# Sums of x, and bias plus projection product, taken from GpSimd to VectorE beside the MLP

## The chip, the cores and the metric

The kernel runs on one core of a Trainium2 chip. Its five engines have their own instruction queues, each worked through in order: TensorE (PE, with its weight loads as PEld), VectorE (DVE), ScalarE (ACT), GpSimd (POOL) and SyncE (SP, which here only issues transfers). The metric is the device time of one execution in microseconds, as the median of several runs.

## The reference, cut to what matters

The input x holds 8 batches of 3008 rows with 256 columns. Each batch goes through a real Fourier transform along the rows, a complex linear layer, a soft threshold and the inverse transform; all rows then go through a two-layer MLP of width 2048.

```python
X = np.fft.rfft(x, axis=1)
Yr = Xr @ w_r - Xi @ w_i + b_r
Yi = Xr @ w_i + Xi @ w_r + b_i
Yr = np.sign(Yr) * np.maximum(np.abs(Yr) - lam, 0.0)   # Yi the same
y = np.fft.irfft(Yr + 1j * Yi, n=3008, axis=1)
h = y.reshape(24064, 256) @ w_in
out = np.maximum(0.01 * h, h) @ w_out
```

## The kernel before

The transform of length 3008 is split into 47 times 64. For a batch `b` there are three parts.

`fwd(b)` does the transform of length 47. It loads x in 7 column groups of 512 (the last 256): two tiles `xa` and `xb` of 120 rows each, the second holding the mirrored rows. `fold(c)` makes the sum (into the tile `xs`) and the difference (in place of `xa`), L249 and L250. For batches 2 to 7, `split` then cuts each of the two into a rounded high part and a rest (`xz`, L258 and L259, on VectorE), `stage_a` multiplies on TensorE, ScalarE copies the product from PSUM, and ScalarE's queue stores it into DRAM (`u_dram`). Two groups are loaded ahead. Batch 0 folds on VectorE, batch 1 has no fold at all (`stage_a1`), so the fold runs on GpSimd for batches 2 to 7: 6 times 7 groups, 84 instructions.

`mid(b)` does the transform of length 64 (`stage_b`), the linear layer (`proj`), the threshold and the first part of the way back (`stage_g`), in 12 pairs per batch. In `proj` three products are made; the first (`ps_k`, of `w_r`) serves both the real and the imaginary part. ScalarE copies it to `kc` (L379), and GpSimd adds it, repeated twice, to the two bias rows: `kb` (L381). Later VectorE adds `kb` to the other two products (`t`, L389), and the threshold follows (L390, L391). This runs 12 times in each of 8 batches, 96 times in all; 84 of these belong to batches 1 to 7.

The MLP works through 47 chunks of 512 rows, in 8 steps each, 376 steps in all. A step has `moe_a` (four products into two PSUM banks of tag `psh`), then the second layer of two steps earlier (`moe_o`, in two halves), then `moe_b` (three more products into the same banks). Between them VectorE has to take sums from those banks: L542 (which needs ScalarE's copy `p1`, L541), L544 and L545 after `moe_a`, L556 after `moe_b`; ScalarE's activations (L555, L558) and cast (L560) and VectorE's L562 then make the operands of the second layer. The first matmul of each product in `moe_b` waits for the reader of what it adds to: the last for L545. Between the steps a chunk's operands are made from the inverse transform (`inverse`, L479 to L492) and `forms` (L504 to L512).

What sets the order: the program emits MLP half steps, and after each the spectral work of the next batches (`fwd(b+1)`, then `mid(b)`) up to the share that is due. A list scheduler with a time model of its own then fixes each engine's queue. The MLP's parts are tied to follow one another on TensorE; the spectral work is placed between them. The first batch's `mid(0)` and `fwd(1)` run ahead of the MLP, in about the first 200 us. Buffers: `xs` has one buffer under the tag `e`, shared with `mid`'s operand; `psf` has two PSUM banks for all spectral products; `kb` has one buffer, which `c` of the threshold also uses.

Of the kernel before, what the change touches and what calls it, by code (L numbers as in the profile page):

```python
# [8 lines left out]
F32 = mybir.dt.float32  # L9
# [11 lines left out]
P = 128  # L21
# [9 lines left out]
def spectral_mlp_kernel(  # L31
# [18 lines left out]
    D = w_r.shape[0]  # L50
# [13 lines left out]
    sb = ctx.enter_context(tc.tile_pool(name="sb", bufs=2))  # L64
    dram = ctx.enter_context(tc.tile_pool(name="dram", bufs=2, space=bass.MemoryType.DRAM))
    ps = ctx.enter_context(tc.tile_pool(name="ps", bufs=1, space=bass.MemoryType.PSUM))
    sync, act, dve, pool = nc.sync, nc.scalar, nc.vector, nc.gpsimd

    def bank(tag, bufs):
        return ps.tile([P, 512], F32, name=tag, tag=tag, bufs=bufs)  # L70

    def products(dst, pairs):

        terms = []
        dst = dst.rearrange("p (s b a) -> p s b a", a=2, b=P)
        for l, r in pairs:
            terms += [(l[0], r[0]), (l[0], r[1]), (l[1], r[0])] if len(l) == 2 else [(l[0], r[0])]
        for i, (a, b) in enumerate(terms):
            b = b.rearrange("p (s a b) -> p s b a", a=2, b=P)
            last = nc.tensor.matmul(dst, a, b, start=(i == 0), stop=(i == len(terms) - 1))  # L80
        return last
# [16 lines left out]
    def flat(t):  # L98
        return t.rearrange("p a b -> p (a b)")
# [120 lines left out]
    def fwd(b):  # L220
        ud = dram.tile([2, NK1, NG * NS, D], F32, name="u_dram", tag="u_dram", bufs=NPRE + 1)
        u_dram[b] = ud
        uv = ud.rearrange("c k (g s) d -> c (k g) (s d)", g=NG)
        x_t, s_t = {}, {}

        def load(c):
            cols = slice(2 * c * D, min(2 * c + 2, NS) * D)
            n = cols.stop - cols.start
            if b < NPRE:
                tag, bufs = (XT, XT1)[b][c]  # L230
                x2 = sb.tile([PA, 2, 2 * D], F32, name="xin", tag=tag, bufs=bufs)
                x_t[c] = [x2[:, h, :n] for h in range(2)]
            else:
                x_t[c] = [
                    sb.tile([PA, 2 * D], F32, name=f"xin{h}", tag="uv"[h], bufs=3 - h)[:, :n] for h in range(2)
                ]
            for h, t in enumerate(x_t[c]):
                if b == 0:
                    (act if h else sync).dma_start(t, x[b, h, :, cols])
                else:  # L240
                    with tc.issue_after(reads[-1].ins):
                        sync.dma_start(t, x[b, h, :, cols])

        def fold(c):
            xa, xb = x_t[c]
            n = xa.shape[1]
            eng = pool if b else dve
            xs = sb.tile([PA, 2 * D], F32, name="xs", tag="e", bufs=1)[:, :n] if b else xs3[:, c % 3, :n]
            eng.tensor_add(xs, xa, xb)  # L249
            eng.tensor_sub(xa, xa, xb)  # L250
            s_t[c] = [(xs,), (xa,)] if b < NPRE else [xs, xa]

        def split(c, h):
            t = s_t[c][h]
            n = t.shape[1]
            z = sb.tile([PA, 2, 2 * D], F32R, name="xz", tag="z", bufs=1)
            xh, xl = z[:, 0, :n], z[:, 1, :n]
            dve.tensor_copy(xh, t)  # L258
            dve.tensor_sub(xl, t, xh.bitcast(F32))  # L259
            s_t[c][h] = (xh, xl)  # L260

        def stage_a(c, h):
            t = x_t[c][h]
            n = t.shape[1]
            pa = (bank("psf", 2) if b else bank("psh", 4))[:PA, :n]
            products(pa, [(consts[f"fa{h}"] if b else consts[f"fa{h}32"], s_t[c][h])])
            t = x_t[c][1 - h]
            cp = act.copy(t, pa)
            if b == 0:
                turned[:] = [cp]  # L270
            st = (act if b else sync).dma_start(uv[h, :, 2 * c * D:2 * c * D + n], t)
            if b == 0:
                written.append(st)

        def stage_a1(c):

            n = x_t[c][0].shape[1]
            pas = [(bank("psf", 2) if c in (4, 5) else bank("psh", 4))[:PA, :n] for _ in range(2)]
            for h in range(2):
                with tc.issue_after(turning[NPAIR - 2].ins):  # L280
                    products(pas[h], [
                        (consts[f"fa{h}32"], (x_t[c][0],)), (consts[f"fa{2 * h}32"], (x_t[c][1],))])
            for h in range(2):
                act.copy(x_t[c][h], pas[h])
                sync.dma_start(uv[h, :, 2 * c * D:2 * c * D + n], x_t[c][h])

        if b == 1:
            for c in range(NX):
                load(c)
                yield 0  # L290
            for c in (0, 1, 2, 3, 6, 4, 5):
                stage_a1(c)
                yield 6 * x_t[c][0].shape[1]
            return

        ahead = 2 if b >= NPRE else NX
        for c in range(ahead):
            load(c)
        yield 4 * CS if b >= NPRE else 0
        fold(0)  # L300
        if b >= NPRE:
            split(0, 0)
        yield 0
        for c in range(NX):
            for h in range(2):
                if h == 0 and c + ahead < NX:
                    load(c + ahead)
                if h == 0 and c + 1 < NX:
                    fold(c + 1)
                stage_a(c, h)  # L310
                if b >= NPRE and (c + h < NX):
                    split(c + h, 1 - h)
                yield 3 * x_t[c][h].shape[1]


    def mid(b):
# [49 lines left out]
        def proj(j):  # L366

            e = e_t.pop(j)
            ps_k = bank("psf", 2) if b else bank("pso", 2)
            ps_y = None if b else bank("psf", 2)  # L370
            for dst, c, w in ((0, 2, "wr"), (0, 1, "wn"), (D, 0, "wd")):
                if c == 1 and b:
                    ps_y = bank("psf", 2)
                products((ps_k if c == 2 else ps_y)[:, dst:dst + D], [
                    (tuple(t[:, a, c, :] for t in e), tuple(t[:, a, :] for t in consts[w]) if b else (consts[w + "32"][0][:, a, :],)) for a in range(NH)
                ])
                if c == 2:
                    kc = sb.tile([P, D], F32, name="kc", tag="kc")
                    act.copy(kc, ps_k[:, :D])  # L379
                    kb = sb.tile([P, 2, D], F32, name="kb", tag="kb", bufs=1)  # L380
                    pool.tensor_add(kb, bias, kc.unsqueeze(1).broadcast_to([P, 2, D]))  # L381
                if c:
                    yield 6 * D
                if c == 2 and b and j:
                    stage_g(j - 1)
                    yield 3 * CS
            t = sb.tile([P, 2, D], F32, name="t", tag="t" if b else "v", bufs=1 if b else 2)
            c = sb.tile([P, 2, D], F32, name="c", tag="kb" if b else "yt", bufs=1)
            dve.tensor_add(flat(t), ps_y, flat(kb))  # L389
            dve.tensor_scalar(c, t, LAMBDA, -LAMBDA, ALU.min, ALU.max)  # L390
            thresholded.append(dve.tensor_sub(t, t, c))  # L391
            zf = z0[j % 3] if b == 0 else sb.tile([P, 2, D], F32, name="zf", tag="zf", bufs=1)
            for i in range(2):
                s = slice(64 * i, 64 * (i + 1))
                act.copy(zf[:64, i, :], t[s, 0, :])
                if b == 0 and j == NPAIR - 1:
                    dve.tensor_scalar(zf[64:, i, :], t[s, 1, :], sign[s, NK1 + j:NK1 + j + 1], None, ALU.mult)
                else:
                    act.mul(zf[64:, i, :], t[s, 1, :], sign[s, NK1 + j:NK1 + j + 1])  # L399
            if b == 0:  # L400
                z_t[j] = (zf,)
                yield 6 * D
                return
            z = sb.tile([P, 2, 2, D], F32R, name="zh", tag="z", bufs=1)
            zh, zl = z[:, 0], z[:, 1]
            act.copy(zh, zf)
            dve.tensor_sub(zl, zf, zh.bitcast(F32))
            z_t[j] = (zh, zl)
            yield 6 * D
# [14 lines left out]
        if b:  # L424
            for s in range(NPAIR):
                if s + 2 < NPAIR:
                    load(s + 2)
                stage_b(s)
                yield 16 * P
                yield from proj(s)  # L430
            stage_g(NPAIR - 1)
            yield 3 * CS
            return
# [240 lines left out]
    bias = const.tile([P, 2, D], F32, name="bias")  # L674
# [166 lines left out]
```

## Time and profile before

Times and the profiled execution:

| | |
|---|---|
| median of 3 runs | 2502.09 us (2500.66 to 2505.65) |
| profiled execution | 2500.07 us, its span 2498.3 us |
| mean granted TensorE clock | 0.995 |
| PE busy | 2431.1 us, 97% |
| VectorE busy | 1896.1 us, 76% |
| ScalarE busy | 1659.1 us, 66% |
| GpSimd busy | 255.3 us, 10%, 192 instructions |

The span is the time from the first to the last instruction on the core; the execution's own time has 1.8 us around it. A busy share is over the whole span. "Idle before" is the time that an engine stood still ahead of an instruction, put down to what released it last.

### The profile page before, as it was taken

To read this page: it belongs to the slowest core of one execution; us is meant where nothing else is said; L and a number is where in the kernel's file an instruction comes from. 1 tells how busy PE (TensorE), PEld (TensorE's weight loads), DVE (VectorE), ACT (ScalarE), POOL (GpSimd) and SP (SyncE) were. 2 spreads that over 40 slices of the span, in tenths; PEclk is the share of its full clock that TensorE was granted. 3 is DMA by queue.
4 is the path that set the end of the run, shared out by engine and by line. 5 is a ranking of instruction groups with operands and counts; after the bars stand their busy time and mean duration, and the time that the engine had idled before them with its cause. 6 is when DMAs were issued, how large, how long until landed. Compare 5 with 4: busy or idle time off the path is not lost.

```text
span 2498.3 us, 42605 instructions
## 1 busy us (share of the span) xinstructions
PE 2431.1 (97%) x16276; PEld 2230.4 (89%) x16276; DVE 1896.1 (76%) x3400; ACT 1659.1 (66%) x3172; POOL 255.3 (10%) x192
## 2 busy tenths in 40 slices
PE   6989999999999999999999999999999999999999
PEld 4579988999889999999999999889999899999998
DVE  7687778777777778777787777877778777777775
ACT  5667765776657776576766777667776677656564
POOL 1200112000110101100011000201002010000000
PEclk8999999999999999999999999999999999999999
DMA  8531123211231113221132111321113211101000
GB/s 272 148 107 50 55 67 96 66 53 42 74 91 56 51 38 88 82 61 47 43 93 82 47 55 39 105 70 51 51 35 109 69 55 51 50 18 33 9 18 18
DMA packets 119904, 165.12 MB, mean 66 GB/s; under 512 B 13597, under 2 KB 69909, under 8 KB 119701
## 3 DMA queue, kind: packets, MB, share of 16 engines
q1 hardware_dynamic: 79112, 115.54, 15.0%
q10 hardware_dynamic: 40589, 46.87, 7.3%
q8 instruction: 128, 2.10, 0.4%
q14 instruction: 75, 0.61, 0.1%
HBM read 86.60 MB, written 75.76 MB: 65 GB/s over the span
## 4 chain that ended last, share of the span: by engine, by line
PE 84%; DVE 7%; ACT 4%; DMA 2%; issue 2%; ACTq 0%; POOL 0%; SPq 0%; DVEq 0%; POOLq 0%
PE pso L576 35%; PE psh L96 32%; PE psf L80 11%; PE psf L479 3%; PE psf L347 2%; PE psh L80 1%; DVE yl L505 1%; DMA u_dram<-xin 1%; DVE gl L562 1%; ACT gf L558 1%; ACT zf L399 1%; DMA u<-u_dram 1%; DVE t L389 0%; DVE gf L545 0%; DVE gf L556 0%
## 5 line engine op out<-in xcount | busy, mean ns | idle before, releaser
L96 PE MATMUL psh<-yh,win_hi 128*128 128x256 f32 x2632 | 740.5, 281 | 23.7 <-DVE gf L545 17.7
L96 PE MATMUL psh<-yl,win_hi 128*128 128x256 f32 x2632 | 725.9, 276 | 0.5 <-DVE yl L505 0.5
L96 PE MATMUL psh<-yh,win_lo 128*128 128x256 f32 x2632 | 726.1, 276 | 0.0
L576 PE MATMUL pso<-gh,wout_hi 128*128 128x512 f32 x1504 | 575.1, 382 | 0.1
L576 PE MATMUL pso<-gl,wout_hi 128*128 128x512 f32 x1504 | 571.2, 380 | 0.6 <-DVE gl L562 0.6
L576 PE MATMUL pso<-gh,wout_lo 128*128 128x512 f32 x1504 | 570.3, 379 | 0.0
L96 PEld LDWEIGHTS psh<-yh,win_hi 128*128 128x128 f32 x2632 | 505.9, 192 | 40.5 <-DVE gf L545 23.3
L562 DVE TENSOR_TENSOR gl<-gf,gh 128x1024 fp32r<-128x1024 f32 x376 | 470.2, 1251 | 92.2 <-ACT gh L560 90.1
L96 PEld LDWEIGHTS psh<-yl,win_hi 128*128 128x128 f32 x2632 | 506.0, 192 | 7.2 <-DVE yl L505 0.7
L96 PEld LDWEIGHTS psh<-yh,win_lo 128*128 128x128 f32 x2632 | 506.7, 193 | 0.1
L560 ACT CAST gh<-gf 128x1024 fp32r<-128x1024 f32 x376 | 394.6, 1050 | 7.2
L556 DVE TENSOR_TENSOR gf<-psh,u 128x512 f32<-128x512 f32 x376 | 258.3, 687 | 181.1 <-PE psh L96 180.6
L558 ACT ACTIVATE gf<-gf 128x768 f32<-128x768 f32 x376 | 318.7, 848 | 65.8 <-DVE gf L556 64.1
L576 PEld LDWEIGHTS pso<-gl,wout_hi 128*128 128x128 f32 x1504 | 284.3, 189 | 41.1 <-DVE gl L562 1.5
L576 PEld LDWEIGHTS pso<-gh,wout_hi 128*128 128x128 f32 x1504 | 285.8, 190 | 29.7 <-ACT gh L560 0.5
L576 PEld LDWEIGHTS pso<-gh,wout_lo 128*128 128x128 f32 x1504 | 285.6, 190 | 28.3
L381 POOL TENSOR_TENSOR kb<-bias,kc 128x512 f32<-128x512 f32 x96 | 142.9, 1489 | 1538.7 <-ACT kc L379 1418.1
L555 ACT ACTIVATE gf<-psh 128x256 f32<-128x256 f32 x376 | 145.1, 386 | 230.8 <-PE psh L96 183.9
L541 ACT COPY p<-psh 128x256 f32<-128x256 f32 x376 | 139.7, 372 | 190.7 <-PE psh L96 188.0
L542 DVE TENSOR_TENSOR u<-psh,p 128x256 f32<-128x256 f32 x376 | 157.7, 419 | 100.5 <-ACT p L541 98.9
L544 DVE TENSOR_TENSOR gf<-psh,u 128x256 f32<-128x256 f32 x376 | 158.7, 422 | 29.3 <-PE psh L96 1.6
L545 DVE TENSOR_TENSOR gf<-psh,gf 128x256 f32<-128x256 f32 x376 | 158.6, 422 | 9.0
(126 smaller groups left out, 3242.6 us busy)
## 6 DMA issues: line engine op xcount, KB each, us to landing
u<-u_dram SPq DMA_DIRECT2D x192, 128.0 KB, 2.7
v_dram<-v ACTq DMA_DIRECT2D x192, 128.0 KB, 2.4
out_dram<-ob SPq DMA_DIRECT2D x94, 256.0 KB, 2.2
vin<-v_dram SPq DMA_DIRECT2D x96, 240.0 KB, 3.4
xin<-x_dram SPq DMA_DIRECT2D x90, 240.0 KB, 3.0
u_dram<-xin ACTq DMA_DIRECT2D x72, 240.0 KB, 2.4
u_dram<-xin SPq DMA_DIRECT2D x24, 240.0 KB, 4.6
raw<-w_out_dram SPq DMA_DIRECT2D x8, 512.0 KB, 4.3
```

The source lines that it names most:

```text
L80: last = nc.tensor.matmul(dst, a, b, start=(i == 0), stop=(i == len(terms) - 1))
L96: mlp[:] = [nc.tensor.matmul(dst, a, b, start=start and i == 0, stop=i == 2, skip_group_check=True)]
L381: pool.tensor_add(kb, bias, kc.unsqueeze(1).broadcast_to([P, 2, D]))
L542: dve.tensor_add(u2, b1[:, hi], p1)
L544: dve.tensor_add(g[:, 3], b2[:, hi], u2)
L545: dve.tensor_add(g[:, 3], b2[:, lo], g[:, 3])
L555: act.activation(g[:, 0], b1[:, lo], AF.Prelu, alpha=SLOPE)
L556: dve.tensor_add(g[:, 1:3], b2.rearrange("p (k n) -> p k n", k=2), u2.unsqueeze(1).broadcast_to([P, 2, HT]))
L558: act.activation(g[:, 1:4], g[:, 1:4], AF.Prelu, alpha=SLOPE)
L560: cp = act.copy(gh, g)
L562: parted[:] = [cp, dve.tensor_sub(gl, g, gh.bitcast(F32))]
L576: mlp[:] = [nc.tensor.matmul(pv, a[:, f, s], r[:, i], start=(f == 0 and j == 0), stop=(f == NF - 1 and j == 2),)]
```

## The change

Two edits. `fold` always runs on VectorE. For batches 1 to 7, `kb` is made by one VectorE instruction that reads the product straight from PSUM, and ScalarE's copy `kc` is gone; batch 0 keeps the copy and the add on GpSimd.

```diff
         def fold(c):
             xa, xb = x_t[c]
             n = xa.shape[1]
-            eng = pool if b else dve
             xs = sb.tile([PA, 2 * D], F32, name="xs", tag="e", bufs=1)[:, :n] if b else xs3[:, c % 3, :n]
-            eng.tensor_add(xs, xa, xb)
-            eng.tensor_sub(xa, xa, xb)
+            dve.tensor_add(xs, xa, xb)
+            dve.tensor_sub(xa, xa, xb)
...
                 if c == 2:
-                    kc = sb.tile([P, D], F32, name="kc", tag="kc")
-                    act.copy(kc, ps_k[:, :D])
                     kb = sb.tile([P, 2, D], F32, name="kb", tag="kb", bufs=1)
-                    pool.tensor_add(kb, bias, kc.unsqueeze(1).broadcast_to([P, 2, D]))
+                    if b:
+                        dve.tensor_add(kb, bias, ps_k[:, :D].unsqueeze(1).broadcast_to([P, 2, D]))
+                    else:
+                        kc = sb.tile([P, D], F32, name="kc", tag="kc")
+                        act.copy(kc, ps_k[:, :D])
+                        pool.tensor_add(kb, bias, kc.unsqueeze(1).broadcast_to([P, 2, D]))
```

## Rows read from the trace of the kernel before

**Rows 1.** The page's first part: busy time, share of the span and instructions of each engine.

```profile
PE 2431.1 (97%) x16276; PEld 2230.4 (89%) x16276; DVE 1896.1 (76%) x3400; ACT 1659.1 (66%) x3172; POOL 255.3 (10%) x192
```

**Rows 2.** Busy time in the six stretches in which `fwd(2)` to `fwd(7)` fold. Columns: the stretch and its length in us; busy us and number of instructions of PE, PEld, DVE, ACT, POOL; granted TensorE clock, DMA share, GB/s.

```profile
355.00:430.00 75.00, 73.45 (x470) 66.75 (x469) 62.85 (x103) 46.90 (x82) 20.69 (x14) 1.00 0.36 103
651.00:736.00 85.00, 79.51 (x499) 73.10 (x498) 68.87 (x117) 50.22 (x88) 17.87 (x14) 0.96 0.33 93
965.00:1040.00 75.00, 74.63 (x486) 68.82 (x485) 60.74 (x105) 46.57 (x82) 16.74 (x14) 1.00 0.35 101
1268.00:1345.00 77.00, 76.59 (x495) 70.57 (x495) 62.03 (x107) 48.65 (x84) 17.78 (x14) 1.00 0.35 102
1571.00:1650.00 79.00, 77.43 (x503) 71.13 (x502) 63.33 (x110) 49.91 (x88) 18.71 (x14) 1.00 0.35 102
1879.00:1954.00 75.00, 74.63 (x486) 68.81 (x485) 61.17 (x105) 46.85 (x82) 17.73 (x14) 1.00 0.37 104
```

**Rows 3.** The same view of one stretch in which a `mid` runs beside the MLP, and of the stretch after the last `mid`, in which only the MLP and the inverse transform are left.

```profile
1040.00:1268.00 228.00, 224.95 (x1595) 212.60 (x1594) 173.04 (x323) 159.57 (x319) 17.02 (x13) 1.00 0.18 52
...
2156.00:2400.00 244.00, 244.00 (x1662) 228.98 (x1661) 175.60 (x308) 148.59 (x263) 0.00 (x0) 1.00 0.09 28
```

**Rows 4.** What PE waited for from 200 to 2400 us: us in total, times, longest.

```profile
PE psh L96 <- DVE gf L545: 12.0, 16, 2.8
PE psf L347 <- DMA u<-u_dram: 7.0, 4, 2.0
PE psf L347 <- issue: 4.0, 2, 2.2
PE psh L96 <- DVE u L542: 3.2, 3, 2.1
```

**Rows 5.** Groups of instructions by line and shape over the whole span: count, busy us and mean ns of one, idle time of the engine before them and its releasers.

```profile
L381 POOL TENSOR_TENSOR kb<-bias,kc 128x512 f32<-128x512 f32 x96 | 142.9, 1489 | 1538.7 <-ACT kc L379 1418.1 <-DVE gl L562 82.1 <-DVE yt L508 18.1
...
L389 DVE TENSOR_TENSOR t<-psf,kb 128x512 f32<-128x512 f32 x96 | 65.7, 685 | 25.6 <-POOL kb L381 12.3 <-PE psf L80 11.2 <-PE psh L96 2.0
L391 DVE TENSOR_TENSOR t<-t,c 128x512 f32<-128x512 f32 x96 | 65.7, 685 | 1.3
...
L249 POOL TENSOR_TENSOR xs<-xin,xin 120x512 f32<-120x512 f32 x36 | 47.4, 1316 | 299.0 <-DVE xz L259 126.9 <-DMA xin<-x_dram 54.2 <-DMA vin<-v_dram 33.3
...
L379 ACT COPY kc<-psf 128x256 f32<-128x256 f32 x84 | 31.2, 372 | 16.9 <-PE psf L80 11.8 <-PE psh L96 1.9 <-ACT gf L555 1.7
...
L249 DVE TENSOR_TENSOR xs<-xin 120x512 f32<-120x512 f32 x6 | 4.2, 692 | 8.7 <-DMA xin<-x_dram 8.6
...
L321 POOL MEMSET zero<- 48x256 f32 x8 | 2.4, 304 | 0.7 <-POOLq L828 0.3
```

**Rows 6.** VectorE's groups by line and shape from 200 to 2156 us, in which GpSimd works beside it; columns as in the group before.

```profile
L562 DVE TENSOR_TENSOR gl<-gf,gh 128x1024 fp32r<-128x1024 f32 x302 | 379.7, 1257 | 68.4 <-ACT gh L560 66.5
...
L510 DVE TENSOR_TENSOR yt<-yc,yt 128x256 f32<-128x256 f32 x38 | 20.6, 543 | 2.5 <-ACT yc L492 1.9
L512 DVE TENSOR_TENSOR yc<-yc,yt 128x256 f32<-128x256 f32 x38 | 19.0, 500 | 0.0
```

**Rows 7.** The same groups from 2156 to 2400 us, in which GpSimd does nothing.

```profile
L562 DVE TENSOR_TENSOR gl<-gf,gh 128x1024 fp32r<-128x1024 f32 x47 | 57.5, 1224 | 15.2 <-ACT gh L560 15.0
...
L510 DVE TENSOR_TENSOR yt<-yc,yt 128x256 f32<-128x256 f32 x6 | 2.5, 420 | 0.1
...
L512 DVE TENSOR_TENSOR yc<-yc,yt 128x256 f32<-128x256 f32 x6 | 2.5, 418 | 0.0
```

**Rows 8.** VectorE's instructions in order of time from 651 us on: start us, length us, engine, line, operation, tiles, shape.

```profile
651.25 1.50 DVE L510 TENSOR_TENSOR yt<-yc,yt 128x256 f32<-128x256 f32 x1
652.68 1.48 DVE L511 TENSOR_TENSOR yc<-yc 128x256 f32<-128x256 f32 x1
...
655.68 0.68 DVE L391 TENSOR_TENSOR t<-t,c 128x512 f32<-128x512 f32 x1
656.29 0.68 DVE L505 TENSOR_TENSOR yl<-yt,yh 128x512 fp32r<-128x512 f32 x1
```

**Rows 9.** GpSimd's instructions in the same stretch, with the idle time before them in brackets.

```profile
651.14 1.33 POOL L249 TENSOR_TENSOR xs<-xin,xin 120x512 f32<-120x512 f32 x1 [9.85 <-DMA xin<-x_dram]
652.55 1.33 POOL L250 TENSOR_TENSOR xin<-xin,xin 120x512 f32<-120x512 f32 x1
```

**Rows 10.** What PE waited for from 651 to 660 us.

```profile
PE psh L96 <- DVE gf L545: 2.8, 1, 2.8
PE psh L96 <- DVE u L542: 2.1, 1, 2.1
```

**Rows 11.** Busy time and granted clock (third number from the right) in and behind that wait; columns as in the second group.

```profile
658.00:662.00 4.00, 3.71 (x17) 3.71 (x18) 1.96 (x4) 1.62 (x4) 0.00 (x0) 0.50 0.00 0
...
655.00:664.00 9.00, 6.19 (x29) 5.82 (x30) 6.41 (x13) 5.48 (x10) 0.00 (x0) 0.62 0.01 2
```

**Rows 12.** What GpSimd waited for over the whole span, the fold's transfers alone.

```profile
POOL xs L249 <- DMA xin<-x_dram: 54.2, 6, 9.9
POOL xs L249 <- DMA vin<-v_dram: 33.3, 2, 21.0
```

**Rows 13.** What VectorE waited for from 200 to 2400 us, two rows of it.

```profile
DVE y L483 <- DMA out_dram<-ob: 9.8, 9, 1.6
...
DVE t L389 <- POOL kb L381: 5.0, 6, 0.8
```

## The prediction

> **What bounds the kernel now.** I read the page's busy times first: PE is busy 97% of the span, VectorE 76%, ScalarE 66%, GpSimd 10% [rows 1]. So the time can only fall where PE waits or its clock is low, and rise where PE is made to wait more. Second, the stretches. In the six that fold, PE stands idle 1.55, 5.49, 0.37, 0.41, 1.57 and 0.37 us (length less busy), 9.8 us in all, with VectorE busy 379 of 466 us, 81% [rows 2]. Beside a `mid` PE loses 3.1 us of 228 with VectorE at 76%; with neither, nothing in 244 us at 72% [rows 3]. The reader is to see that PE's losses are small wherever one looks. Third, PE's waits: from 200 to 2400 us, L545 costs 12.0 us in 16 waits and L542 3.2 us in 3; the other large rows are transfers that the change doesn't touch [rows 4]. In 302 steps (the count of L562 [rows 6]) VectorE is thus late 19 times, 6.3%. Last, whether GpSimd has part in them: two VectorE instructions on 256 columns take 1.50 and 1.48 us at 651 us [rows 8], where their mean is 0.42 us without GpSimd [rows 7], and two GpSimd sums run at just that time [rows 9]. PE then waits 2.1 and 2.8 us [rows 10].
>
> **The change part by part.** All terms are made against the profiled execution's own 2500.07 us (span 2498.3 and 1.8 around it); the median of the runs lies 2.0 us above.
>
> *The first 200 us.* Batch 0 keeps its path and batch 1 has no fold, so nothing is added or removed there: 0.
>
> *The folds.* 84 instructions leave GpSimd and come to VectorE: 72 of 512 columns and 12 of 256. VectorE's own fold of batch 0 takes 0.692 us against GpSimd's 1.316 [rows 5]. VectorE starts instructions of that size 0.61 us apart (655.68 to 656.29 [rows 8]), so 72 x 0.61 = 44 us of its queue, and 12 at about half, 4: together 48 us. What goes: the stretching of VectorE by GpSimd. For three lines alone, mean with GpSimd less mean without: L562 (1257 - 1224) x 302 = 10.0 us, L510 (543 - 420) x 38 = 4.7, L512 (500 - 418) x 38 = 3.1: 17.8 us [rows 6, 7]. Other lines add to it, so I take 18 as a lower bound. Net, VectorE gets at most 30 us more in 466 us: (379 + 30) / 466 = 88%. It isn't the bound on average; what counts is how often the extra time lies ahead of an L545 that PE is near to needing. I price this by the share of steps that are late already: 30 x 0.063 = +1.9 us. The bounds are 0 (all of it falls in VectorE's idle time) and 30 (every microsecond passes to PE).
>
> The stretch at 651 us is priced by itself. There 1.08 + 1.06 = 2.1 us of stretch goes, and the pair of sums, whose data has just landed, comes in its place with 2 x 0.61 = 1.2 us: -1.0 us of PE's 4.9 us. Behind the wait the granted clock is 0.50 from 658 to 662 us, the lower of the two levels (1.2 GHz), after PE's two waits [rows 10], and 0.62 from 655 to 664 us [rows 11]: 0.38 x 9 = 3.4 us lost, the idle part counted twice. A shorter wait may or may not keep the clock; bounds 0 and -3.4, I take the middle, -1.7.
>
> *The fold in VectorE's queue.* On GpSimd the fold waits for its load with nothing behind it that matters: 6 times for `xin` itself, 54.2 us, and twice for a transfer ahead of it in the queue [rows 12]. On VectorE everything of the MLP stands behind it. Where the queue's order has the fold before its data has landed, VectorE stops, and L542 to L545 with it. The trace doesn't show this wait. From below it is 0: at 651 us VectorE was busy past the landing. From above, VectorE's nearest wait for a transfer is 9.8 / 9 = 1.1 us [rows 13], PE's for `u` 7.0 / 4 = 1.75 us [rows 4]; with 8 folds, 14 us. I take 0, as at 651 us, and make the other end a rival. The loads themselves are issued by SP in the old order, when a store frees their buffer; nothing is moved past anything there.
>
> *The bias add.* 84 GpSimd instructions (1.489 us each) and 84 ScalarE copies of 0.372 us, 31.2 us, go [rows 5]. VectorE gets 84 adds of 512 columns with one input in PSUM. L389 has just this shape and inputs, 0.685 us, no longer than L391 from SBUF alone [rows 5]. At 0.61 us apart they take 51 us of VectorE over seven `mid`s. By the share of late steps: 51 x 0.063 = +3.2 us (bounds 0 and 51). The PSUM bank is now held until VectorE comes round to the add instead of ScalarE's copy; two yields of other work lie before that bank's next product, so I add nothing for it. Below nothing: ScalarE's 31 us lie ahead of other copies, of which L541 leads to L542. PE's waits for L542 are 3.2 us [rows 4]; I take half as gone, -1.6 (bounds 0 and -3.2). VectorE's 5.0 us of waits for `kb` [rows 13] go too: 5.0 x 0.063 = -0.3.
>
> The Trainium skill ("Perfetto Trace Analysis", Optimizing Scalar/DVE Operations) puts the fixed cost of a VectorE access at about 60 ns for SBUF and 125 ns for PSUM. An estimate from that page would be 84 x 65 ns = 5.5 us more on VectorE, 0.3 us of time by the share above; the equal means of L389 and L391 show none of it.
>
> *What stays.* The memset of 48 rows, 0.30 us, runs once per `mid` on GpSimd [rows 5]; it reads nothing, and I give it 0.
>
> **Sum.** 1.9 - 1.0 - 1.7 + 3.2 - 1.6 - 0.3 = +0.5 us. On the profiled execution 2500.6, on the median 2502.6; the terms are no finer than a microsecond, so I say 2502. Its own range is 2498 to 2506: within it lie the doubled or vanished terms of the queue (5.1 us) with the clock either way.
>
> **The rivals.** *Faster: the order takes the sums in, and the stretch alone was the harm.* The list scheduler knows a VectorE instruction's place in the queue, and need not know of the stretching. Speaking for it: three of six fold stretches already lose only 0.4 us [rows 2], and the three that lose more have 8.6 us of idle time together, 5.5 of them where the two stretched instructions stand. If all six came to 0.4, 9.8 - 2.3 = 7.5 us go, with the clock's 3.4 it is 10.9; with ScalarE's 1.6 gained and half of the bias add's 3.2 paid it stays 10.9: 2502.1 - 10.9 = 2491. Against it: VectorE at 88% beside the folds, where even 72% to 76% is not free of waits.
>
> *Slower: VectorE stops for the fold's load.* Place: the first two folds of each batch, and others whose data lands just in time. Price: 8 stops of 1.75 us, 14 us. Where VectorE lost 2.1 us, PE lost 4.9; take three quarters of the stops as reaching PE, 10.5 us: 2502.1 + 10.5 = 2513 with the sum's remainder. It decides from about 8 us of waits at L249. For it: the loads do land last before their fold. Against it: between the landing and the fold's first use VectorE often has work of the MLP queued.
>
> *Slower: VectorE has too much.* The same page and section of the skill advises to hand work to ScalarE or GpSimd where VectorE is saturated, though it warns that GpSimd shares a read port with it. As a mechanism here: at 88% late steps double in the fold stretches and rise by half beside the `mid`s. PE's 15.2 us of waits [rows 4] would become about 24: 2502 + 9 = 2511. This needs bursts, since no stretch comes to 100%.
>
> *The change does less than it says* is hardly open: both edits name their engine; only the memset stays.
>
> **How the numbers follow.** About 0.2%, 5 us, is what a measurement of this kernel can tell from no change. No change (2502): 0.37. Faster (2491, with its own range 2486 to 2497): 0.35. Slower: 0.28, of which the stop 0.15 and the load 0.13. To leave out no more than two in ten, the range reaches into the middle of both sides: 2489 to 2512.
>
> **What would show it.** Right: GpSimd with 12 adds and 8 memsets left; L510 and L562 at 0.42 and 1.22 us everywhere; VectorE busy near 1896 + 48 + 51 - 18 = 1977 us or somewhat more (busy time counts 0.69 and not 0.61, which adds 12); ScalarE 31 us lower. PE's idle time in the six fold stretches near 8 us, and its waits for L545 near 14. Wrong: a row "DVE xs waits for DMA xin" beyond 8 us (the stop); waits for L545 above 20 us (the load); fold stretches that all lose under 1 us with the clock at 1.00 throughout (the faster case).

## The result and the profile after

The changed kernel takes 2525.19 us (median of 6 runs, 2520.99 to 2527.54) against 2503.81 us of the kernel before: a ratio of 1.0077, 95% interval 1.0067 to 1.0087. It is slower by 0.8%. 2502 us with a range of 2489 to 2512 was predicted; the time lies above the range, and the nearest of the cases is the rival "VectorE stops for the fold's load" (2513). The profiled execution took 2524.32 us, its span 2522.5 us, mean granted clock 0.992.

The page's first part of the kernel after, as in [rows 1]:

```profile
PE 2441.1 (97%) x16276; PEld 2237.0 (89%) x16276; DVE 1955.2 (78%) x3568; ACT 1638.0 (65%) x3088; POOL 23.9 (1%) x24
```

The same 16276 matmuls are busy 10.0 us longer, and the span less PE's busy time has risen from 67.2 to 81.4 us, by 14.2: together the 24.2 us by which the span is longer. Most of the busy part is the clock: 0.5% of 2498.3 is 12.5 us, 0.8% of 2522.5 is 20.2, so 7.7 us more are lost to it (the clock is printed to a thousandth, which leaves 1 to 2 us open).

Where PE stands idle: the six stretches that fold, and the whole steady part (columns as in [rows 2]; the limits are shifted with the kernel's own time).

```profile
355.00:440.00 85.00, 78.42 (x481) 70.56 (x480) 66.14 (x121) 46.83 (x81) 0.00 (x0) 0.96 0.33 95
660.00:745.00 85.00, 78.50 (x492) 70.89 (x491) 70.13 (x129) 49.68 (x89) 0.00 (x0) 0.98 0.33 93
965.00:1053.00 88.00, 87.28 (x569) 80.30 (x569) 75.73 (x138) 55.44 (x98) 0.00 (x0) 1.00 0.33 94
1285.00:1360.00 75.00, 72.88 (x466) 66.30 (x466) 63.85 (x115) 46.40 (x81) 0.00 (x0) 1.00 0.34 96
1590.00:1667.00 77.00, 74.62 (x481) 68.14 (x481) 65.96 (x122) 48.85 (x87) 0.00 (x0) 1.00 0.36 101
1895.00:1972.00 77.00, 75.55 (x487) 68.88 (x486) 65.81 (x120) 46.19 (x81) 0.00 (x0) 1.00 0.35 98
...
200.00:2420.00 2220.00, 2177.55 (x14926) 2035.08 (x14924) 1736.88 (x3198) 1461.23 (x2767) 0.00 (x0) 1.00 0.20 58
```

The stretches lose 6.58, 6.50, 0.72, 2.12, 2.38 and 1.45 us, 19.7 in all, where [rows 2] lost 9.8. (Cut alike in both kernels, from 5 us ahead of a batch's first fold to 10 us behind the start of its last, they lose 16.9 and 9.8.) From 200 to 2420 us PE is idle 2220 - 2177.55 = 42.5 us; the same row of the kernel before:

```profile
200.00:2420.00 2220.00, 2189.77 (x15084) 2050.71 (x15084) 1694.93 (x3056) 1493.94 (x2871) 231.64 (x173) 1.00 0.21 59
```

There it is 30.2. So 12 of the 14 us are lost in the steady part, where the change works. VectorE is no fuller than was forecast: 407.62 of the stretches' 487 us, 84%.

What VectorE waits for from 200 to 2450 us (us in total, times, longest):

```profile
DVE gf L558 <- PE psh L96: 147.2, 149, 3.7
DVE u L544 <- ACT p L543: 81.7, 129, 1.8
...
DVE xs L248 <- DMA xin<-x_dram: 17.6, 7, 4.2
DVE kb L379 <- PE psf L80: 16.9, 19, 1.8
```

Neither of the last two rows has a counterpart before. (Lines have moved: L248 is the fold's first sum, L379 the bias add; L544, L546 and L547 answer to L542, L544 and L545 of before, L558 to L556, L564 to L562.) The first is the row that the prediction named as the sign of the stop, "beyond 8 us".

How one stop looks, VectorE's timeline at 376 us (start, duration, engine, line; in brackets the idle time before):

```profile
376.85 0.68 DVE L258 TENSOR_TENSOR xz<-xs,xz 120x512 fp32r<-120x512 f32 x1
377.44 0.42 DVE L544 TENSOR_TENSOR u<-psh,p 128x256 f32<-128x256 f32 x1
382.06 0.69 DVE L248 TENSOR_TENSOR xs<-xin,xin 120x512 f32<-120x512 f32 x1 [4.20 <-DMA xin<-x_dram]
382.67 0.42 DVE L546 TENSOR_TENSOR gf<-psh,u 128x256 f32<-128x256 f32 x1
383.00 0.68 DVE L249 TENSOR_TENSOR xin<-xin,xin 120x512 f32<-120x512 f32 x1
383.60 0.42 DVE L547 TENSOR_TENSOR gf<-psh,gf 128x256 f32<-128x256 f32 x1
```

The planned order has the batch's second fold between L544 and L546, the sums that free TensorE's banks. The fold stands at the head of the queue for 4.20 us until its load has landed, and L546 and L547 stand behind it. What PE waited for from 376 to 412 us:

```profile
PE psh L96 <- DVE gf L547: 3.6, 1, 3.6
PE psf L80 <- DVE xz L258: 1.7, 2, 1.1
```

And why the load is late: what SP's queue waited for from 360 to 390 us, and its issues from 372 us.

```profile
...
SPq L466 <- DMA v_dram<-v: 10.1, 1, 10.1
```

```profile
375.61 0.34 SPq L466 DMA_DIRECT2D vin<-v_dram  x1
376.01 1.59 SPq L460 DMA_DIRECT2D vin<-v_dram  x1
377.65 0.40 SPq L466 DMA_DIRECT2D vin<-v_dram  x1
378.15 0.35 SPq L242 DMA_DIRECT2D xin<-x_dram  x1
```

SP's queue holds for 10.1 us at a `vin` load that must wait for the last store of the `mid` before, and the `xin` load comes behind three `vin` loads, at 378.15; it ends the fold's wait 3.9 us later. Such a stop, 2.0 to 4.2 us long, stands at the second fold of each of the six batches; a seventh wait, of 0.5 us, comes later in one of them. On GpSimd the wait at the second folds is in [rows 12] as the two rows put down to `vin`, 33.3 us, and nothing that TensorE needs was queued behind it.

### The profile page after: what moved, and what is told of

Its sections match the earlier page's. It is cut to its first block, busy times and chain, and to the rows that moved or that the text cites. A ratio compares the mean times of both kernels' runs of the same rounds, so it can differ in the third digit from the quotient of the medians.

```text
span 2522.5 us, 42186 instructions
## 1 busy us (share of the span) xinstructions
PE 2441.1 (97%) x16276; PEld 2237.0 (89%) x16276; DVE 1955.2 (78%) x3568; ACT 1638.0 (65%) x3088; POOL 23.9 (1%) x24
## 4 chain that ended last, share of the span: by engine, by line
PE 81%; DVE 7%; DMA 4%; ACT 4%; issue 2%; SPq 1%; ACTq 0%; POOL 0%; DVEq 0%; POOLq 0%
PE pso L578 33%; PE psh L96 30%; PE psf L80 11%; PE psf L481 3%; PE psf L346 3%; DMA xin<-x_dram 1%; DVE gl L564 1%; PE psh L80 1%; ACT gf L560 1%; DVE yl L507 1%; DMA u_dram<-xin 1%; DVE gf L558 1%; DMA u<-u_dram 1%; ACT gh L562 1%; DMA raw<-w_out_dram 0%
## 5 line engine op out<-in xcount | busy, mean ns | idle before, releaser
L564 DVE TENSOR_TENSOR gl<-gf,gh 128x1024 fp32r<-128x1024 f32 x376 | 459.5, 1222 | 71.1 <-ACT gh L562 69.3
L562 ACT CAST gh<-gf 128x1024 fp32r<-128x1024 f32 x376 | 394.7, 1050 | 7.5
L558 DVE TENSOR_TENSOR gf<-psh,u 128x512 f32<-128x512 f32 x376 | 258.6, 688 | 157.7 <-PE psh L96 156.9
L544 DVE TENSOR_TENSOR u<-psh,p 128x256 f32<-128x256 f32 x376 | 158.1, 421 | 87.8 <-ACT p L543 87.0
L546 DVE TENSOR_TENSOR gf<-psh,u 128x256 f32<-128x256 f32 x376 | 158.9, 423 | 26.6 <-PE psh L96 1.8
L547 DVE TENSOR_TENSOR gf<-psh,gf 128x256 f32<-128x256 f32 x376 | 158.8, 422 | 8.4
L481 PEld LDWEIGHTS psf<-ga,vin 120*128 120x128 f32 x832 | 109.7, 193 | 6.3 <-issue 2.1
```

Source lines behind the costliest of these rows:

```text
L481: nc.tensor.matmul(py[:, o:o + P], vin[:, c, i, s], consts["ga"][:, c, :], start=True, stop=True)
L544: dve.tensor_add(u2, b1[:, hi], p1)
L546: dve.tensor_add(g[:, 3], b2[:, hi], u2)
L547: dve.tensor_add(g[:, 3], b2[:, lo], g[:, 3])
L558: dve.tensor_add(g[:, 1:3], b2.rearrange("p (k n) -> p k n", k=2), u2.unsqueeze(1).broadcast_to([P, 2, HT]))
L562: cp = act.copy(gh, g)
```

## The experiments

Three theories stood against each other. *The stop*: what is lost is VectorE standing at the fold's load. *The load*: each added VectorE instruction costs by its time. *The bank*: the bias add, read straight from PSUM, waits for its product in VectorE's queue and holds the bank until then. A fourth had to be kept in view: the planner lays out another order for any edit, and that alone moves the time. The expectations below use letters: A is the stop, B that the bias add costs most, C the order, D the load, E the bank (E1 its wait, E2 that it is held longer). Ratios are to the kernel before, timed on the same chip, with 95% intervals.

### One part alone

Folds on VectorE, the bias add as before:

```diff
-            eng = pool if b else dve
...
-            eng.tensor_add(xs, xa, xb)
-            eng.tensor_sub(xa, xa, xb)
+            dve.tensor_add(xs, xa, xb)
+            dve.tensor_sub(xa, xa, xb)
```

> Only the first edit: the folds of batches 2 to 7 on VectorE, the bias add left on ScalarE and GpSimd. Theory A (VectorE stops for the second fold's load, one stop of 2.0 to 4.2 us per batch, 17 us in all in the changed kernel, with the fold's bursts beside it): most of the 21 us is here, 2515 to 2525 us, and the trace has 5 or 6 waits of VectorE for the load of x. Theory B (the bias add in VectorE's queue costs the time): 2500 to 2507 us here. Theory C (any change to a queue reshuffles the list scheduler's order, and the loss has no place): no sum, so this run and the next need not add up to 21 us.

Measured: 1.0049 (1.0036 to 1.0062). Then the bias add alone, with the second hunk of the change and the folds on GpSimd:

> Only the second edit: the bias add of batches 1 to 7 on VectorE from PSUM, the folds left on GpSimd. Theory A: 2498 to 2507 us, no wait of VectorE for the load of x. Theory B: 2515 to 2525 us. Theory C: anything between, not adding up with the other run.

Measured: 1.0031 (1.0021 to 1.0040). The parts add up: 0.49% and 0.31% make 0.80%, the whole change has 0.77%. Each is worse than the prediction had it. The folds alone lie where theory A put them, with its six stops; the bias add alone (2512.46 us) lies above what A gave it (2507) and below what B did (2515).

### The folds without their stop

The stop is taken away in two ways. First, in batches 2 to 7 the fold reads only the tile that comes first and never the one that comes late; its instructions keep their number and length:

```diff
-            eng = pool if b else dve
...
-            eng.tensor_add(xs, xa, xb)
-            eng.tensor_sub(xa, xa, xb)
+            dve.tensor_add(xs, xa, xa if b else xb)
+            dve.tensor_sub(xa, xa, xs if b else xb)
```

> Folds of batches 2 to 7 on VectorE, bias add as before, and the fold reads only the first of the two x tiles (xs = xa + xa, then xa - xs), so that it doesn't wait for the second, which lands late; the output is not the reference's in these batches. Same number, size and operands in SBUF of VectorE's instructions as in the run with the folds alone (ratio 1.0049). Theory A (the stop for the late load): ratio 0.999 to 1.002. Theory D (VectorE's extra 48 us in the fold stretches delay the sums that TensorE waits for, load or not): ratio 1.004 or more.

Measured: 1.0010 (1.0000 to 1.0020). Second, the late tile gets a third buffer (its tag `v` is shared with two tiles of `mid`, which get it too), on the kernel with the folds alone:

```diff
-  ... name=f"xin{h}", tag="uv"[h], bufs=3 - h)
+  ... name=f"xin{h}", tag="uv"[h], bufs=3)
...
-  v = sb.tile([P, 2, D], F32, name="v", tag="v" if b else "y")
+  v = sb.tile([P, 2, D], F32, name="v", tag="v" if b else "y", bufs=3 if b else 2)
...
```

> Folds alone on VectorE, with the third buffer, bias add as before, output complete. Theory A: below the 1.0049 without the buffer and near the 1.0016 of the kernel before with the buffer: 1.001 to 1.003. If the stops were not the cost, 1.005 or more.

Measured: 1.0010 (1.0002 to 1.0019). The row to look at is VectorE's wait for the load; in the kernel with the folds alone (200 to 2450 us) it is

```profile
DVE xs L248 <- DMA xin<-x_dram: 15.8, 6, 3.2
```

and the two kernels without the stop have no such row. So without the six stops of 15.8 us in all the time is 0.49 - 0.10 = 0.39%, about 9.8 us, lower, and the 84 fold instructions, net of what leaves GpSimd, then cost next to nothing.

Is that the price of the stop? PE's idle time in the six fold stretches, cut alike in every kernel as above, can tell. Their sums for the folds alone, the folds with the third buffer, the whole change, and the whole change with the third buffer (below):

```profile
sum 444.00, PE 432.65 PEld 393.75 DVE 378.08 ACT 266.48 POOL 0.00; mean PE 72.11 PEld 65.62 DVE 63.01 ACT 44.41 POOL 0.00
...
sum 436.00, PE 426.83 PEld 391.86 DVE 379.35 ACT 267.04 POOL 0.00; mean PE 71.14 PEld 65.31 DVE 63.23 ACT 44.51 POOL 0.00
...
sum 446.00, PE 429.07 PEld 388.98 DVE 375.26 ACT 263.16 POOL 0.00; mean PE 71.51 PEld 64.83 DVE 62.54 ACT 43.86 POOL 0.00
...
sum 436.00, PE 425.58 PEld 389.41 DVE 375.76 ACT 264.18 POOL 0.00; mean PE 70.93 PEld 64.90 DVE 62.63 ACT 44.03 POOL 0.00
```

Length less PE's busy time, beside the same for 200 to 2420 us (g1 and g2, the change with another bias add, follow further down):

| kernel | stops at second folds, us | PE idle in the fold stretches, us | PE idle from 200 to 2420, us | ratio |
|---|---|---|---|---|
| before | none | 9.8 | 30.2 | 1 |
| e1, folds alone | 15.8 | 11.4 | 36.3 | 1.0049 |
| f1, one tile | none | 12.1 | 32.6 | 1.0010 |
| g3, third buffer | none | 9.2 | 32.9 | 1.0010 |
| after | 17.1 | 16.9 | 42.5 | 1.0077 |
| e4, third buffer | none | 10.4 | 36.8 | 1.0065 |
| g1 | 15.0 | 10.7 | 33.5 | 1.0015 |
| g2, third buffer | none | 9.2 | 32.6 | 1.0015 |

Where the stops go, PE's idle time in these stretches falls by 6.5 us in the whole change, by 1.5 in the last pair, and for the folds alone by 2.2 with the third buffer and not at all with one tile. Of the 6.1 us of idle time that the folds alone add between 200 and 2420 us, 1.6 lie in the fold stretches; the rest lies where that edit has no instruction. So the stop is shown, and so is idle time of PE behind it; that the stop itself costs the 0.39% is not. The same stops go with 0.39%, 0.12% and nothing in the three pairs, and an order alone moves the time by more (below).

The buffers by themselves, on the kernel before, are the control:

> Control: the kernel before with the same third buffer, folds on GpSimd. Theory A: the earlier load helps little where GpSimd does the waiting, 2496 to 2505 us. If it gains as much as the changed kernel does, the buffer is worth something for itself and theory A is not shown by the other run.

Measured: 1.0016 (1.0006 to 1.0026), 2508.66 us and above the range expected: the third buffer, with the other order that comes of it, costs this much with no stop of VectorE to remove. Against this control the folds on VectorE (1.0010) cost nothing. And on the whole change:

> The changed kernel with a third buffer under the tag v, which the second x tile of a group shares with the tile that mid stores to DRAM. The second tile of the second group then need not wait for the last store of mid, and its load stands ahead of the vin loads in SP's queue. Theory A: the stops at the second fold go (under 4 us in all instead of 17) and 8 to 14 us come back, 2511 to 2517 us. Theory B: no gain beyond 3 us. Theory C: a move of either sign that is not tied to the fold stretches.

Measured: 1.0065 (1.0051 to 1.0079), 2521.81 us: 3 us better than the change, and above the range that theory A gave. The stop is gone, and PE's idle time from 200 to 2420 us falls by 5.6 us, all of it in the fold stretches (table above):

```profile
200.00:2420.00 2220.00, 2183.18 (x14974) 2043.74 (x14973) 1745.43 (x3211) 1466.89 (x2778) 0.00 (x0) 0.99 0.21 59
```

The profiled execution gives this back at the clock (0.989 against 0.992, 0.3% of the span, 8 us). Most of that lies in the first 200 us, ahead of the folds that the change moves; the granted clock is the third number from the right, in the whole change and with the third buffer:

```profile
0.00:200.00 200.00, 166.47 (x723) 112.92 (x724) 153.63 (x265) 122.51 (x235) 23.89 (x24) 0.95 0.56 169
...
0.00:200.00 200.00, 164.40 (x674) 110.07 (x675) 144.74 (x253) 116.87 (x223) 24.95 (x24) 0.92 0.56 167
```

That is 0.03 x 200 = 6 us. Two of the five runs with the third buffer have a mean clock of 0.992 and take 2518.57 and 2520.01 us; the two of the whole change at 0.992 (on another chip) take 2524.32 and 2526.06. At one clock, on two runs of each, taking the stops away would thus be worth some 6 us, as much as the idle time that goes; over all runs it is 3.

### No folds at all

To see what the folds cost on GpSimd, batches 2 to 7 skip them:

```diff
+            if b:
+                s_t[c] = [xa, xa]
+                return
```

> The kernel before without the folds of batches 2 to 7 at all (split and the products take the first x tile alone; the output is not the reference's in these batches), bias add as before. GpSimd then stretches VectorE only by the bias adds. It gives the price of the folds on GpSimd: theory A and D alike say 0.995 to 0.998, since 5 us of waits and 3 us of low clock stand at the stretched sums at 651 us. If it is 1.000, what GpSimd did to VectorE cost nothing in the end.

Measured: 0.9950 (0.9938 to 0.9963), 12.5 us below before. So the sums on GpSimd were not free; what of it is contention and what late data isn't separated. It is also about the most that a move of them can gain. And against this kernel the folds on VectorE without their stop (1.0010) cost 0.60%, 15 us: they come cheap only beside the folds on GpSimd, so *the load* is not refuted for the folds. (A part of the 0.60%, too, can be the data that the products then wait for.)

### The bias add from ScalarE's copy

VectorE makes the same add, for the same batches, but from the copy `kc`, which stays on ScalarE:

```diff
-  pool.tensor_add(kb, bias, kc.unsqueeze(1).broadcast_to([P, 2, D]))
+  (dve if b else pool).tensor_add(kb, bias, kc.unsqueeze(1).broadcast_to([P, 2, D]))
```

> Bias add of batches 1 to 7 on VectorE, but from ScalarE's copy in SBUF, folds on GpSimd: the copy frees the PSUM bank as before, VectorE has the same extra time, and ScalarE keeps its 31 us. Theory D: ratio 1.003 to 1.005. Theory E: 1.000 to 1.001.

Measured: 0.9977 (0.9967 to 0.9987): faster than the kernel before and than either theory had it, and no other kernel that makes the whole output is faster. VectorE's group by line and shape in the kernel that reads PSUM, and in this one:

```profile
L380 DVE TENSOR_TENSOR kb<-bias,psf 128x512 f32<-128x512 f32 x84 | 57.4, 684 | 17.5 <-PE psf L80 16.6
```

```profile
L381 DVE TENSOR_TENSOR kb<-bias,kc 128x512 f32<-128x512 f32 x84 | 57.6, 686 | 13.3 <-ACT kc L379 13.2
```

The same 84 instructions of the same length: from PSUM they cost 0.31%, from the copy they gain 0.23%. So VectorE's time is not what the bias add costs, and *the load* falls here.

Is it the wait, or the bank? This kernel keeps ScalarE's copy, which now nobody reads, and adds from PSUM:

```diff
-                    pool.tensor_add(kb, bias, kc.unsqueeze(1).broadcast_to([P, 2, D]))
+                    if b:
+                        dve.tensor_add(kb, bias, ps_k[:, :D].unsqueeze(1).broadcast_to([P, 2, D]))
+                    else:
+                        pool.tensor_add(kb, bias, kc.unsqueeze(1).broadcast_to([P, 2, D]))
```

> Bias add on VectorE from PSUM as in the run with the add alone (ratio 1.0031), but ScalarE's copy is kept, with no reader: the add then waits for ScalarE's copy, as the faster form from SBUF does (0.9977), while the PSUM bank is still held until VectorE has read it. Theory E1 (the add waiting for TensorE at the head of VectorE's queue is what costs): ratio 0.997 to 0.999. Theory E2 (the bank held longer is what costs): 1.002 to 1.004.

Measured: 0.9999 (0.9986 to 1.0011), between the two. Its add waits longest of all in VectorE's queue, since the trace shows it behind the copy (whole group, columns as above):

```profile
L382 DVE TENSOR_TENSOR kb<-bias,psf 128x512 f32<-128x512 f32 x84 | 57.4, 684 | 31.7 <-ACT kc L379 31.7
```

31.7 us of waits and a bank that is read still later cost nothing, where 17.5 us cost 0.31%. Neither the sum of waits nor the time to the bank's reading puts the kernels in the order of their times. *The bank* is not shown, and in its plain form speaks against these rows.

One more try at the load: the kernel before, with a second add of the same size on VectorE whose result nobody reads.

```diff
+                    if b:
+                        dve.tensor_add(spare, bias, kc.unsqueeze(1).broadcast_to([P, 2, D]))
...
+    spare = const.tile([P, 2, D], F32, name="spare")
```

> The kernel before, unchanged but for one more VectorE add of 128x512 beside each bias add of batches 1 to 7, from the same SBUF tiles into a tile that nobody reads. Theory D (VectorE's time itself): ratio 1.002 to 1.005, as with the bias add on VectorE (1.0031). Theory E (the cost is that the add waits for TensorE's product at the head of VectorE's queue, 15.3 us in 18 waits, or holds the PSUM bank): 1.000 to 1.001.

Measured: 1.0060 (1.0044 to 1.0076). It looked like a price for the instructions, but it doesn't measure that: both adds start when `kc` is there, and each slows the other. VectorE's takes 1104 ns instead of 686, GpSimd's 1688 instead of 1489 [rows 5]:

```profile
L381 POOL TENSOR_TENSOR kb<-bias,kc 128x512 f32<-128x512 f32 x96 | 162.1, 1688 | 1541.4 <-ACT kc L379 1493.4 <-DVE gl L564 22.4 <-DVE yt L510 11.4
...
L383 DVE TENSOR_TENSOR spare<-bias,kc 128x512 f32<-128x512 f32 x84 | 92.8, 1104 | 15.1 <-ACT kc L379 14.8
```

So it can't price the instructions alone: its cost is partly contention that neither kernel has.

### Both, with the copy kept

The whole change with the add from the copy, and the same with the third buffer:

> Both parts on VectorE, the bias add from ScalarE's copy. If the parts add up, 1.0049 and 0.9977 give 1.0026. If the two VectorE loads meet (theory D), 1.005 or more.

Measured: 1.0015 (1.0004 to 1.0026).

> The same with the third buffer under the tag v, which took the stops at the late load away (but let the clock drop more often). Theory A with adding parts: f1's 1.001 and 0.9977 give 0.999; with the clock drops of the run with the buffer, up to 1.003.

Measured: 1.0015 (1.0006 to 1.0024). Most of the change's 0.77% goes with the read from PSUM; putting the folds on VectorE still gives back what the add had gained (0.9977 to 1.0015), stop or no stop. The first of the two has its six stops (15.0 us), the second none, and their times are the same: here the stop has no price that could be measured.

### Another order for all

The share of spectral work that is due after each half step is shifted by 2%, so that the planner lays out other queues from the same instructions:

```diff
-         work = frac / 0.95 * sum(s.total for s in streams)
+         work = frac / 0.93 * sum(s.total for s in streams)
```

On the kernel before, on the change, on the bias add from PSUM and on the bias add from the copy:

> Control for order alone: the kernel before, with the share of the spectral work that is due after each half step of the MLP raised by 2% (0.95 to 0.93 in one line). No instruction is added or removed; the list scheduler's order shifts. Theory C (order noise as large as the effects): ratio off 1.000 by more than 0.003 either way. Theories A and E (effects with a place): 0.998 to 1.002.

> The changed kernel in the same shifted order. Theories A and E: slower than p_before by 0.006 to 0.009, with 5 or 6 stops of VectorE at the fold's load again. Theory C: the loss may vanish or double.

> Bias add on VectorE straight from PSUM, folds on GpSimd, in the shifted order. Theory E (the add from PSUM costs): slower than p_before by 0.002 to 0.004. Theory C: any sign.

> Bias add on VectorE from ScalarE's copy, folds on GpSimd, in the shifted order. Theory E: faster than p_before by about 0.002, and 0.004 to 0.006 faster than p_e2. Theory C: any sign; then the difference between the two ways to the bias add was order alone.

Measured, against the unshifted kernel before: 1.0063 (1.0050 to 1.0075), 1.0127 (1.0112 to 1.0143), 1.0074 (1.0062 to 1.0087) and 1.0037 (1.0025 to 1.0050). An order alone moves the time by 0.63%, nearly as much as the change and beyond what theories A and E allowed; that is theory C's own sign. Within the shifted order the effects keep their signs: the change 1.0127 / 1.0063, +0.64%, with a stop at each second fold again (18.3 us in 8 waits); the add from PSUM +0.11%, which with both intervals (some 0.18% together) is not told from nothing; the add from the copy -0.26%. Between the two ways to the bias add lie 0.37% here and 0.54% in the first order.

### All of them by one number

PE's idle time from 200 to 2420 us, 2220 less PE's busy time in the row that is shown above for three kernels (one execution each), beside the ratio, which is one of medians:

| kernel | idle us | ratio |
|---|---|---|
| f2_no_folds | 24.4 | 0.9950 |
| h1_copy_and_psum | 29.0 | 0.9999 |
| f4_kb_from_sbuf | 29.8 | 0.9977 |
| before | 30.2 | 1 |
| f1, g3 (folds, no stop) | 32.6, 32.9 | 1.0010, 1.0010 |
| g1, g2 | 33.5, 32.6 | 1.0015, 1.0015 |
| e5_before_more_buffers | 33.1 | 1.0016 |
| p_f4 | 35.6 | 1.0037 |
| e2_kb_only | 36.2 | 1.0031 |
| e1_folds_only | 36.3 | 1.0049 |
| e4_more_buffers | 36.8 | 1.0065 |
| p_before | 38.3 | 1.0063 |
| f3_add_alone | 39.7 | 1.0060 |
| after | 42.5 | 1.0077 |
| p_e2 | 43.1 | 1.0074 |
| p_after | 53.7 | 1.0127 |

From before to the last row 23.5 us of idle time go with 1.27%, 31.8 us. The mean clock of that kernel is 0.992 against 0.995, 7.6 us, which is nearly the rest. PE's row of one stretch thus puts these kernels nearly in the order of their times, but not to a few microseconds: the add from the copy has the idle time of the kernel before and takes 0.23% less, and each of the two parts alone has 36 us, 0.18% apart.

## Why the prediction was wrong

- **What bounds the kernel** was right: PE's waits and its clock make up nearly the whole difference of 24.2 us, 14.2 of idle time and about 7.7 of clock.
- **The fold in VectorE's queue** is the step that failed first: "I take 0, as at 651 us". It measured 17.6 us of waits at L248; from each stop's beginning to 8 us behind its end PE is idle 7.4 us in all, and the third buffer takes 6.5 us of idle time out of the fold stretches. What that is in time stays open between nothing and 0.39%. The rival had the mechanism and the sign right, and was given 0.15; its price (10.5 us) took three quarters of the stops as reaching PE, where at most 7.4 of 17.6 us, 42%, did. It was wrong to take VectorE's being busy at one landing as typical: 651 us is the first fold of a batch, and at first folds VectorE stops in no batch. All long stops are at second folds. [rows 12] doesn't keep the two apart. Of GpSimd's 54.2 us for `xin`, four waits (9.6 to 9.9 us) stand at first folds and two at fourth ones, and VectorE has none at either. The wait that passed on is that of GpSimd's second folds, 11.2 to 21.0 us in every batch, put down to `vin` in two and to an instruction of VectorE in four. The longest:

```profile
674.91 1.28 POOL L249 TENSOR_TENSOR xs<-xin,xin 120x512 f32<-120x512 f32 x1 [21.03 <-DMA vin<-v_dram]
```

  "The loads themselves are issued by SP in the old order" was true, and is the reason that they came late.
- **The clock** at 651 us, -1.7 us, was not gained: the first two fold stretches have 0.96 and 0.98 after the change, where [rows 2] has 1.00 and 0.96.
- **The folds' time and the stretch** were right in their sum: 1.9 - 1.0 - 1.7 = -0.8 us forecast, and without the stop +0.10% (2.5 us, from 0 to 5) measured. That is near, and partly luck: GpSimd's folds cost 12.5 us in all and VectorE's, without their stop, 15, so the harm that went and the cost that came were both larger than priced.
- **The rival "faster"** had a true part: without folds at all 0.50% goes. But the sums have to be made, and on VectorE they cost what their absence from GpSimd frees.
- **The bias add** is the second step that failed: "by the share of late steps: 51 x 0.063 = +3.2", less 1.6 and 0.3, so +1.3 us. It measured 0.31%, 7.8 us. The term was not just too small. The price per VectorE microsecond was the wrong model, since the same microseconds from the copy gain 0.23%, 5.8 us. Nor did the -1.6 us come: PE's waits for L542 (L544 after) went from 3.2 us [rows 4] to 2.7. "I add nothing for" the bank was neither confirmed nor refuted.
- **The rival "VectorE has too much"** gave a time near (2511) for a reason that the runs don't bear out: waits for L547 are 14.3 us from 200 to 2400, against 12.0 [rows 4] and the "above 20" that it needed. What it and the sum missed among PE's waits in the kernel after is the row for ScalarE's `eh`, 2.3 us before:

```profile
PE psh L96 <- DVE gf L547: 14.3, 18, 3.6
PE psf L80 <- ACT eh L361: 5.8, 4, 3.1
```

- **The signs**: GpSimd keeps 12 adds and 8 memsets; the sums of `forms` and the last one of the MLP are back at the lengths of [rows 7], from 200 to 2156 us:

```profile
L564 DVE TENSOR_TENSOR gl<-gf,gh 128x1024 fp32r<-128x1024 f32 x299 | 365.3, 1222 | 45.9 <-ACT gh L562 44.4
L512 DVE TENSOR_TENSOR yt<-yc,yt 128x256 f32<-128x256 f32 x37 | 15.5, 418 | 0.4
L514 DVE TENSOR_TENSOR yc<-yc,yt 128x256 f32<-128x256 f32 x37 | 15.4, 417 | 0.0
```

  VectorE is busy 1955.2 us (1977 or more forecast), ScalarE 21 us less (31 forecast), both short of the forecast. So the harm by GpSimd to these lines went as described, and the time rose all the same. The idle time of the fold stretches, "near 8", was 19.7.
- The Trainium skill ("Perfetto Trace Analysis", Optimizing Scalar/DVE Operations) has a higher fixed cost for VectorE at PSUM than at SBUF. The two groups of the bias add, 684 ns from PSUM and 686 from SBUF, show none; the difference between these kernels is not in the instruction.

**What stays open**: what the stop costs in time, and why the add from PSUM costs more than the same add from the copy. The kernels differ in ScalarE's load, in who frees the bank and in the order that the planner makes of both. An order by itself moves the time by up to 0.63%, and the cost of the add from PSUM was 0.31% in one order and 0.11% in another. That some of it is the order's luck is likely, and not shown; the same holds for the folds alone, whose added idle time lies mostly outside the fold stretches. An order held fixed over these kernels would settle it and was not tried.

## What to carry to other kernels

Before work is moved from an idle engine to a busy one, read what the idle engine waited for at that work, instruction by instruction: a wait that cost nothing there can stop everything queued behind it on the new one, as at the second folds here, and the total of the waits doesn't say which of them will. Move first what has its data at hand (the add from a copy that was there anyway gained 0.23%). A buffer that takes such a stop away has a price of its own (0.16% here), so set the one against the other. Judge a change of a few tenths of a per cent in a planned kernel only beside a control in which the order alone is changed.

## What was not expected of the hardware

The same wait of TensorE is followed by another clock in different kernels. Near 1120 to 1135 us three of them have one wait of 3.1 us for `eh`, with PE busy 10.00 us of the 10 before the slice in which it begins (in the third kernel the wait begins in the slice before the one shown). The slice that holds the wait's end (columns as in [rows 2]), in the bias add from PSUM, in the whole change, and in the bias add from the copy:

```profile
1120.00:1130.00 10.00, 6.88 (x40) 6.49 (x39) 7.63 (x17) 6.28 (x14) 0.00 (x0) 0.83 0.09 26
```

```profile
1130.00:1140.00 10.00, 6.88 (x32) 6.42 (x32) 7.06 (x14) 6.32 (x13) 0.00 (x0) 0.66 0.09 26
```

```profile
1120.00:1130.00 10.00, 8.24 (x59) 7.84 (x60) 6.07 (x11) 5.48 (x11) 0.00 (x0) 1.00 0.08 23
```

The granted clock is 0.83, 0.66 and 1.00: part of the stretch at the lower of the two levels (1.2 GHz) in two kernels, none in the third. Which of them falls was not told apart by PE's rows ahead of it, so the clock's share of a wait can be bounded but wasn't forecast.

Second, two adds that read SBUF at the same time, one on VectorE and one on GpSimd, slowed VectorE's from 686 to 1104 ns and GpSimd's from 1489 to 1688: the harm is larger on the faster engine.
